# Block-causal attention with a Mish MLP: batch 0's attention from one f32 load per pair of heads, chunks of 192 tokens sharing PSUM banks, and more operations with a choice of engine

## The chip, the core and the metric

The kernel runs on one core of a Trainium2 chip. Such a core has TensorE (PE, matrix products into PSUM, with its weight loads PEld), VectorE (DVE), ScalarE (ACT), GpSimd (POOL) and SyncE (SP, which here issues every DMA). Each engine works through its own instructions in order and waits for the others at semaphores. The metric is the device time of one execution, in microseconds (us): 1071.83 for the kernel before, the median of 3 runs (1071.18 to 1075.56).

## What is computed

Eight batches of eight heads of attention over 576 tokens, with a mask of blocks of 64, and then an MLP over all 4608 tokens. Everything comes in float32, except that the two weights arrive as float64.

```python
scores = np.matmul(q, k.transpose(0, 1, 3, 2)) / np.sqrt(64)   # 8 x 8 x 576 x 576
mask = block_i >= block_j                                      # blocks of 64
scores = np.where(mask, scores, -1e9)
scores = scores - np.max(scores, axis=-1, keepdims=True)
attn = np.exp(scores)
attn = attn / (np.sum(attn, axis=-1, keepdims=True) + 1e-09)
x = np.matmul(attn, v)                # tokens x 512 after the heads are joined
h = x @ w_in                          # 512 -> 2048
g = h * np.tanh(log1p(exp(h)))        # Mish
out = g @ w_out                       # 2048 -> 512
```

## The kernel before

**Number formats.** A float32 operand is mostly split into a high and a low float16 part (`_hi`/`_lo`, `_h`/`_l`), and a product is made of three float16 ones: high by high, high by low, low by high. Some of the attention at the start is done with float32 operands on TensorE instead ("wide"). Scales that are powers of two keep the float16 parts in range: one per pair of heads for q and k (`scales`, L822), one per batch for v (`scale_x`, L686), one per group of columns for the weights (`pow2`, L448).

**Tiles.** A batch's 576 tokens are two tiles, `HALVES`, of 384 and 192 tokens. For each tile and head, `attend` (L934) does this in order:

- TensorE makes the scores with keys on the partitions, into one of two PSUM buffers `ss` (`scores(0)`, L948 to L954).
- ACT or DVE copies a first part to `mt`, and DVE takes the larger of that and the rest (`copy` L977, `larger` L989). POOL reduces over the partitions (L1021), and DVE or ACT writes the negated maximum as a row of `QB` (L1028 or L1035).
- TensorE adds a second product to the same `ss`, which subtracts the maximum (`scores(1)`), and in the float16 form also adds the low part.
- ACT takes the exponential into `pe` (L1046), POOL clears the masked corners (L1057), and for float16 ACT or DVE and then DVE split it into `p_hi` and `p_lo` (L1064, L1069, L1075).
- TensorE multiplies with v into the one PSUM bank `u` (`values` L1085; L1092 in float32, L1103 to L1105 in float16). A column of ones in v gives the row sums.
- ACT or DVE reads the sums, DVE takes the reciprocal and weighs (L1126 to L1152), and the result is split to `xt_hi` and `xt_lo` (L1163 to L1171).

When all eight heads of a tile are split, SP issues transposing DMAs (`Tile.turn`, L1206) to `x_hi` and `x_lo`. `Tile.m1` (L1217) makes the first MLP product: 16 chunks of 128 columns, 12 matmuls each, into one of three PSUM banks `acc`; ACT then writes Mish of it to `Et` (L1262), a buffer of five slots for four chunks each. `Tile.split` makes `Gt`, high and low, from a slot (L1291 to L1304). `Tile.m2` (L1316) makes the second product in four chunks of 48 matmuls, evacuates each (L1357 or L1364) and stores it (L1387).

**Loads.** `load_pair` (L733) loads q, k and v of two heads. For batch 0's first tile ("own", four pairs) they go in float32 to parts of the still unused `Et`, with k laid out twice with zeros in the other head's rows, so that each head's score product runs over all 128 rows. All other pairs, batch 0's second tile included, use two ring sets: q and k are squared and summed for the scale (ACT, L811), split (L842 to L857) and sent by 12 DMAs to the layout that the products need (L876). The first nine pairs loaded (`WIDE = 9`: four own, four for batch 0's second tile, one of batch 1) keep v and the exponentials in float32.

**Other parts at the start.** `batch` (L652) sums the squares of the batch's v for `scale_x`: four DMAs one after the other into one buffer `VL`, each followed by a square on ACT (L670, L676), then one reduction on POOL and a few DVE operations (up to L689). Every weighing waits for that. `weight` (L489) takes the float64 weights apart: DVE builds float32 from the integer words (L528, L545), ACT squares them for the scale (L556), and the high and low parts are made. For `w_in`'s first three groups (`PEW = (3, 0)`) the low part is the difference of two TensorE products with an identity (L609, L610), which `make_identity` and a negating ACT instruction (L479) prepare ahead of everything else.

**The order.** No engine order is written out by hand. Every operation is handed to a planner (`Plan.add`) with an engine, an estimated duration, its predecessors and the buffers that it takes and frees; some may go to a second engine (`other=`). `Plan.go` simulates the engines with these estimates, taking the ready operation with the earliest due time (table `DUE`), and `Plan.order` runs it backwards and forwards and keeps the best. The instructions are then emitted in the planned order, which fixes each engine's order; semaphores keep the data right. So an estimate that is too short shows as a wait in the trace, and every change of an operation can shift the order of all of them.

Of the kernel before, what the change touches and what calls it, by code (L numbers as in the profile page):

```python
# [19 lines left out]
P = 128  # L20
D = 64
EPS = 1e-9
# [7 lines left out]
    "w": ((198, 45.5, 93.5, 196.5), (118, 220.5, 212.5, 283)),  # L30
    "batch": (209, 220, 278.5, 419.5, 570, 584.5, 680, 822.5),
    "load": (
        (68, 178.5, 94, 89.5),
        (30.5, 24, 165.5, 75.5),
        (143, 130.5, 114.5, 381.5),
        (249, 231.5, 537, 626),
        (450, 465, 506, 532),
        (588, 502.5, 635.5, 628.5),
        (601, 778.5, 735, 673.5),
        (770, 742, 753.5, 656.5),  # L40
        (1259, 954, 806.5, 722.5),
    ),
    "tile": (
        (-10, 235, 68, 43, 118, 37, 41.5, 27.5,
         62.5, 140, 114, 81, 57, 122, 242.5,
         124, 242.5, 120, 204.5, 123.5, 192, 191.5),
        (183.5, 167.5, 87, 61, 129, 80.5, 91, 168.5,
         187.5, 187.5, 115, 163, 265.5, 268.5, 150,
         152, 228.5, 207, 210, 253, 206, 251),
        (103, 130, 155, 132.5, 215, 161, 223.5, 254,  # L50
         188, 203, 201, 270, 399.5, 239.5, 212,
         236, 333.5, 253, 340.5, 375.5, 275.5, 297),
        (253, 168.5, 125.5, 198.5, 289.5, 223, 331.5, 201.5,
         270.5, 394, 316, 368, 286, 369, 296.5,
         511, 308, 562.5, 417.5, 301.5, 373.5, 497.5),
        (232, 318.5, 267, 318, 322.5, 342.5, 487, 377.5,
         415.5, 371.5, 407.5, 319.5, 372.5, 377, 435,
         367.5, 415.5, 399.5, 433, 405.5, 368, 381),
        (328.5, 234, 438.5, 423, 666.5, 634.5, 798.5, 750.5,
         354, 429, 449.5, 442.5, 669.5, 602.5, 621,  # L60
         451.5, 411, 455.5, 533, 469, 648, 604.5),
        (474, 527, 530.5, 473, 536.5, 440, 425.5, 417.5,
         444, 541, 539.5, 524, 546.5, 716, 589,
         645, 449, 529.5, 520, 558, 710, 554),
        (380.5, 532.5, 342.5, 384, 451.5, 504.5, 630.5, 609,
         554, 495.5, 586.5, 512, 660.5, 538, 660.5,
         526, 612.5, 544.5, 692.5, 752.5, 760.5, 719),
        (481, 516, 610, 701.5, 676, 702, 588, 666.5,
         622, 748.5, 705, 739.5, 812.5, 655.5, 692,
         758, 790.5, 750.5, 855, 753.5, 751.5, 828.5),  # L70
        (683.5, 611.5, 574, 555.5, 764.5, 884.5, 506.5, 776,
         585, 615, 733.5, 611.5, 700.5, 680, 625,
         723, 945.5, 630.5, 737, 824, 666, 700),
        (585, 586, 612, 666.5, 620, 811.5, 578, 809,
         599.5, 541, 612.5, 626.5, 682.5, 781, 569.5,
         668.5, 655, 724.5, 657.5, 594.5, 814, 665),
        (781, 620.5, 638, 598.5, 699, 685, 692, 535,
         744.5, 796, 710, 762, 990.5, 631.5, 568,
         884, 869.5, 886, 735.5, 917, 1007, 823),
        (638.5, 1084.5, 660.5, 1071.5, 884, 798.5, 888.5, 766.5,  # L80
         586.5, 780.5, 618, 585, 843.5, 643.5, 933.5,
         766, 646.5, 875, 595, 775.5, 807, 983),
        (736.5, 605, 640.5, 609.5, 734.5, 726.5, 837, 818.5,
         882.5, 881, 857.5, 741, 963, 902, 1124.5,
         1161.5, 996, 738, 735, 794, 766, 751.5),
        (797, 835, 1111, 713.5, 806, 783.5, 943, 780.5,
         868.5, 936, 874.5, 882.5, 849.5, 863, 1069.5,
         1038, 1039, 975.5, 930, 958, 1087.5, 817.5),
        (779, 851, 790, 618.5, 759.5, 896, 933, 783,
         853, 997.5, 1080, 949, 1101, 1129, 1002.5,  # L90
         1131.5, 1065, 950, 955, 943, 989.5, 784.5),
# [4 lines left out]
class Op:  # L96


    def __init__(self, eng, us, emit, after, take, free, due, other):

        us, self.work = us if isinstance(us, tuple) else (us, 0.0)
        self.eng, self.us, self.emit = eng, us, emit
        self.ways = {eng: (us, emit)}
        if other:
# [17 lines left out]
class Plan:  # L122
# [7 lines left out]
    LAT, LATPE, OWN = 0.15, 0.2, 0.06  # L130
# [10 lines left out]

    def part(self, kind, *at):

        self.due = DUE[kind]
        for i in at:
            self.due = self.due[i]

    def add(self, eng, us, emit, after=(), take=(), free=(), other=None, table=None):
        self.ops.append(Op(eng, us, emit, after, take, free, self.due, other))
        self.ops[-1].table = table  # L150
        return self.ops[-1]

    def lat(self, a, b):
        if a.eng == "sp":
            return self.BEGIN + a.work + self.DONE
        if a.eng != b.eng or len(a.ways) > 1 or len(b.ways) > 1:
            return self.LATPE if a.eng == "pe" else self.LAT
        return 0.0 if a.eng == "pe" else self.OWN

    def go(self, due, back=False):  # L160
# [14 lines left out]
        while events:  # L175
            now = events[0][0]
            while events and events[0][0] <= now:
# [11 lines left out]
                for x in getattr(o, after):  # L189
                    j = x.i  # L190
                    lat = self.lat(x, o) if back else self.lat(o, x) * (o.eng != "sp")
# [59 lines left out]
    def order(self):  # L251
# [6 lines left out]
        _, end, _ = self.go([o.due for o in ops])  # L258
        best = None
        for _ in range(self.ROUNDS):  # L260
# [23 lines left out]
def products(ns, full=False, rows=128):  # L284

    if full:
        return sum(n / 600 + 0.07 - min(n, 320) / 9000 for n in ns), sum(n * rows / 32 for n in ns)
# [11 lines left out]
def pool(n):  # L299
    return 0.4 + n / 230  # L300
# [8 lines left out]
def attention_moe(  # L309
# [43 lines left out]
    firsts = []  # L353
    for i in range(NP):
        e = Et.rearrange("p a b c -> p (a b c)")[:, i * 1542 : (i + 1) * 1542]
        e, h = e[:, 0:Q0], e[:, Q0:]
        m = {
            "QF": e[:, 0:Q0].unsqueeze(1).to_broadcast([P, 2, Q0]),
            "KF": h[:, 0:768].rearrange("p (a s) -> p a s", a=2),
            "VF": h[:, 768 : 768 + 6 * (D + 1)].rearrange("p (c f) -> p c f", c=3),  # L360
            "Q": e[:, 0:Q0],
        }
        nc.gpsimd.memset(m["KF"][D:P, 0], 0.0)
        nc.gpsimd.memset(m["KF"][0:D, 1], 0.0)
        for j in (0, P + 1):
            nc.gpsimd.memset(m["VF"][:, :, j : j + 1], 1.0)
        firsts.append(m)
    sets = []
    for i in range(2):
        shapes = {  # L370
            "QA": [P, 2, S],
            "QB": [D + 1, 2, S],
            "KA": [P, 2, KW],
            "KB": [D + 1, 2, KW],
# [3 lines left out]
        w = 10 * (D + 1)  # L378
# [5 lines left out]
        m["VF"] = m["V"].bitcast(F32).rearrange("p (c f) -> p c f", c=5)  # L384
        nc.gpsimd.memset(m["KB"][D : D + 1], MSC)
        nc.gpsimd.memset(m["KA"][:, :, S:KW], 0.0)
        nc.gpsimd.memset(m["KB"][0:D, :, S:KW], 0.0)
        for j in (0, P + 1):
            nc.gpsimd.memset(m["VF"][:, :, j : j + 1], 1.0)
        nc.gpsimd.memset(m["VF"][64:P, 4, 1 : 1 + P], 0.0)  # L390
# [26 lines left out]
    dv, tt = room(2, "dv", [P, 6]), room(2, "tt", [P, 3, D])  # L417
    ql, kl = room(1, "ql", [P, S])[0], room(1, "kl", [P, S])[0]
# [4 lines left out]
    PW = (768, 1024)  # L423
    pe = [const.tile([P, w], F32, name=f"pe{i}") for i, w in enumerate(PW)]
    p_hi = [const.tile([P, w], F16, name=f"p_hi{i}") for i, w in enumerate(PW)]
    p_lo = [const.tile([P, w], F16, name=f"p_lo{i}") for i, w in enumerate(PW)]
# [14 lines left out]
    for t in pe[1], p_hi[1], p_lo[1]:  # L441
        nc.gpsimd.memset(t[:, 896:1024], 0.0)
# [26 lines left out]

    PEW = (3, 0)
# [5 lines left out]
    make_identity(nc, ident)  # L478
    nc.scalar.mul(minus, ident, -1.0)  # L479
# [9 lines left out]
    def weight(which, wait, room_free):  # L489
# [11 lines left out]
        last = [None] * len(raws)  # L501
        done = []
        for g in range(NG):
# [6 lines left out]
            for r in range(0, nrow, per):  # L510
# [12 lines left out]
                    [last[i]] + wait,  # L523
# [26 lines left out]
                last[i] = a  # L550
# [31 lines left out]
                other=(  # L582
# [5 lines left out]
                ),  # L588
            )
            if g < PEW[which]:  # L590
# [8 lines left out]
                    [sc] + scaled[-2],  # L599
# [52 lines left out]
    def batch(b):  # L652
# [13 lines left out]
        for i in range(4):  # L666
            d = add(
                "sp",
                dma(P * n * 4),
                lambda i=i: nc.sync.dma_start(out=flat, in_=src[:, i * n : (i + 1) * n]),  # L670
                [last.get(2)],
            )
# [3 lines left out]
                lambda i=i: nc.scalar.activation(  # L676
                    flat, flat, AF.Square, accum_out=T[:, i : i + 1]
                ),
                [d] + old,
# [11 lines left out]
        new["sx"] = add("dve", 0.6, scale_x, [red])  # L691

# [34 lines left out]


    WIDE = 9
    pair_ends = []  # L730
    last = {}

    def load_pair(b, p, q0, q1, k1, i, wait, own):  # L733
# [6 lines left out]
        nq = q1 - q0  # L740
        rows = slice(p * P, (p + 1) * P)
        nfull, rest = k1 // P, k1 % P
        nck = nfull + (rest > 0)
        wide = len(pair_ends) < WIDE
        if own:
            ts = (
                (m["Q"], qT[b, rows, q0:q1], []),
# [744 lines left out]
```

## Time and profile before

| | |
|---|---|
| time, median of 3 runs | 1071.83 us |
| the profiled execution | 1073.09 us |
| its span, first to last instruction | 1071.3 us |
| PE busy | 1009.7 us, 94% |
| DVE busy | 739.8 us, 69% |
| ACT busy | 771.2 us, 72% |
| POOL busy | 268.7 us, 25% |
| mean granted TensorE clock | 0.971 |

The profile gives each instruction's start, its duration and what ended the idle time ahead of it. On TensorE, matmuls overlap: the duration of one holds its way through the array, so a row of equal matmuls starts far more often than one lasts. The distance between starts is what a matmul costs in a dense row. The granted clock is the share of TensorE's full clock that it was given; at 0.5 a matmul takes twice as long.

### The profile page before, as it was taken

The page shows a single profiled execution, that of the slowest core. Times are in us where ns is not written, and L with a number is a line of the kernel's source. Part 1 is how long each engine was busy: PE and PEld are TensorE (multiplying, and loading weights), DVE is VectorE, ACT ScalarE, POOL GpSimd, SP SyncE. Part 2 cuts the span into 40 slices and gives each one's busy share as a digit, 9 for nine tenths or more (in the row PEclk, how much of TensorE's full clock was granted, in tenths as well). Part 3 has the DMA queues.
Part 4 walks back from the last instruction along what each step waited for, and adds up shares of the span by engine and source line. Part 5 has one row for each costly group of instructions (what it writes and reads, how often), then busy time and mean ns, then how long its engine had stood idle before and what let it go on. Part 6 is the DMA issues. An engine that isn't in the chain of part 4 may idle for free. (4 is left out here: it accounts for less than half of the span.)

```text
span 1071.3 us, 25657 instructions
## 1 busy us (share of the span) xinstructions
PE 1009.7 (94%) x9958; PEld 766.2 (72%) x9958; DVE 739.8 (69%) x1872; ACT 771.2 (72%) x1239; POOL 268.7 (25%) x410
## 2 busy tenths in 40 slices
PE   2888989989999999999999999999999998999998
PEld 1466767777776687777767687677778686767778
DVE  3888888785987578757885678746887578833500
ACT  2557887766988679867877789758887688735521
POOL 4242332241232033312431122212332133301000
PEclk7867999999999999999999999999999999999999
DMA  7767643342434433340435233441434342220100
GB/s 253 215 208 185 198 119 86 95 111 77 98 78 110 107 72 77 106 110 25 105 100 128 64 74 96 113 102 28 105 91 110 91 94 71 50 45 8 31 15 23
DMA packets 126200, 103.78 MB, mean 97 GB/s; under 512 B 51328, under 2 KB 112256, under 8 KB 126080
## 3 DMA queue, kind: packets, MB, share of 16 engines
q1 hardware_dynamic: 126080, 102.16, 36.5%
q8 instruction: 78, 1.28, 0.5%
q14 instruction: 42, 0.34, 0.1%
HBM read 56.10 MB, written 9.44 MB: 61 GB/s over the span
## 5 line engine op out<-in xcount | busy, mean ns | idle before, releaser
L1331 PE MATMUL acc<-Gt,wo_h 128*128 128x192 f16 (+1 forms) x2048 | 385.8, 287 | 1.9 <-ACT Et L1262 1.1
L1237 PE MATMUL acc<-x_lo,wi_h 128*128 128x192 f16 (+1 forms) x1024 | 295.0, 288 | 3.2 <-DMA x_lo<-xt_lo 3.2
L1237 PE MATMUL acc<-x_hi,wi_h 128*128 128x192 f16 (+1 forms) x1024 | 295.1, 288 | 2.0 <-ACT Et L1262 1.3
L1237 PE MATMUL acc<-x_hi,wi_l 128*128 128x192 f16 (+1 forms) x1024 | 295.0, 288 | 0.0
L1331 PE MATMUL acc<-Gt,wo_l 128*128 128x192 f16 (+1 forms) x1024 | 293.8, 287 | 0.0
L1021 POOL PARTITION_ALL_REDUCE mr<-mt x128 | 199.6, 1567 | 300.9 <-DVE mt L992 265.6
L1237 PEld LDWEIGHTS <-wi_h 128*128 128x128 f16 x2048 | 192.2, 98 | 77.4 <-issue 10.6
L1331 PEld LDWEIGHTS <-wo_h 128*128 128x128 f16 x2048 | 188.2, 98 | 51.2 <-issue 1.8
L1262 ACT ACTIVATE Et<-acc,bv 128x384 f32<-128x384 f32 (+1 forms) x256 | 125.5, 498 | 91.0 <-PE acc L1237 89.1
L992 DVE TENSOR_TENSOR mt<-mt,ss 128x192 f32<-128x192 f32 (+3 forms) x448 | 127.6, 297 | 13.6 <-ACT mt L979 9.2
L1304 DVE SCALAR_TENSOR_TENSOR Gt<-Et,bv,Gt 128x1536 f16<-128x1536 f32 (+1 forms) x64 | 91.5, 1431 | 54.2 <-ACT Gt L1291 54.0
L1331 PEld LDWEIGHTS <-wo_l 128*128 128x128 f16 x1024 | 100.0, 98 | 34.5 <-issue 1.3
L1237 PEld LDWEIGHTS <-wi_l 128*128 128x128 f16 x1024 | 100.4, 98 | 33.7 <-issue 1.2
L1046 ACT ACT_TABLE_LOAD x86 | 110.3, 1283 | 18.6 <-PE ss L954 8.2
L1046 ACT ACTIVATE pe<-ss,pv 128x768 f32<-128x768 f32 (+1 forms) x120 | 113.2, 956 | 7.9 <-PE ss L954 5.4
L1075 DVE TENSOR_TENSOR p_lo<-pe,p_hi 128x768 f16<-128x768 f32 (+1 forms) x108 | 113.4, 1051 | 4.5 <-ACT p_hi L1064 3.5
L1057 POOL MEMSET pe<- 64x64 f32 (+1 forms) x192 | 34.4, 210 | 318.1 <-ACT pe L1046 287.1
L1262 ACT ACT_TABLE_LOAD x87 | 111.6, 1283 | 1.5
L954 PE MATMUL ss<-QB,KB 65*128 65x192 f16 (+5 forms) x512 | 67.0, 254 | 29.9 <-POOL pv L819 13.0
L1103 PE MATMUL u<-V,p_hi 128*128 128x65 f16 x810 | 85.4, 194 | 2.1 <-DVE tt L1152 2.1
L1105 PE MATMUL u<-V,p_lo 128*128 128x65 f16 x810 | 84.7, 194 | 0.8 <-DVE p_lo L1075 0.6
L1104 PE MATMUL u<-V,p_hi 128*128 128x64 f16 x810 | 85.3, 193 | 0.0
(107 smaller groups left out, 1391.0 us busy)
## 6 DMA issues: line engine op xcount, KB each, us to landing
VL<-in_v_dram SPq DMA_DIRECT2D x32, 288.0 KB, 3.3
kl<-in_k_dram SPq DMA_DIRECT2D x32, 288.0 KB, 3.2
wo_l<-in_w_in_dram SPq DMA_DIRECT2D x8, 1024.0 KB, 5.7
Gt<-in_w_out_dram SPq DMA_DIRECT2D x16, 512.0 KB, 4.0
ql<-in_q_dram SPq DMA_DIRECT2D x28, 288.0 KB, 3.4
QA<-xh SPq DMA_DIRECT2D x112, 72.0 KB, 2.2
VL<-in_v_dram SPq DMA_DIRECT2D x27, 256.0 KB, 3.0
out_dram<-ot SPq DMA_DIRECT2D x32, 192.0 KB, 2.1
```

Of the source, the lines that this page charges most:

```text
L954: nc.tensor.matmul(ss[:, col : col + q1 - qs], lhsT=k_, rhs=q_, start=x == 0 and col % 512 == 0, stop=True, skip_group_check=True,)
L992: nc.vector.tensor_max(t, t, sv(ss_[A.slot % NSS]))
L1021: lambda: nc.gpsimd.partition_all_reduce(mr[rm][:, 0:n], mt[rm][:, 0:n], P, RED.max),
L1046: lambda: nc.scalar.activation(*spread(pe[rm], ss_[A.slot % NSS]), AF.Exp, scale=st.get("esc", D ** -0.5)),
L1075: lambda: nc.vector.tensor_sub(p_lo[rm][:, 0:W], pe[rm][:, 0:W], p_hi[rm][:, 0:W]),
L1103: nc.tensor.matmul(o, lhsT=h, rhs=vh, start=j == 0 and z == 0, stop=False)
L1104: nc.tensor.matmul(o[:, 0:D], lhsT=h, rhs=vo, start=False, stop=False)
L1105: nc.tensor.matmul(o, lhsT=l, rhs=vh, start=False, stop=end)
L1237: nc.tensor.matmul(pt[:, 0:n], lhsT=w[:, d, f * P : (f + 1) * P], rhs=x[:, d, :], start=d == 0 and z == 0, stop=d == NP - 1 and z == 2,)
L1262: nc.scalar.activation(Et[:, (self.i * NG + g) % NE, j, 0:n], acc_[c.slot % NACC][:, 0:n], AF.Mish, scale=fc[:, 0, g : g + 1])
L1304: lambda g_hi=g_hi, g_lo=g_lo, ev=ev: nc.vector.scalar_tensor_tensor(out=g_lo, in0=ev, scalar=self.s_g, in1=g_hi, op0=ALU.mult, op1=ALU.su ...
L1331: nc.tensor.matmul(pt[:, 0:n], lhsT=w[:, f, o * P : (o + 1) * P], rhs=g, start=f == 0 and z == 0, stop=f == NF - 1 and z == 2,)
```

## The change

It has these parts.

1. **Batch 0 wholly from own loads.** The own pairs now load all 576 tokens of q, k and v, and serve both tiles. The four ring loads for batch 0's second tile, with their splits and crossing DMAs, are gone, and `WIDE` with them: batch 1's first pair is float16. All of batch 0's products with own data are float32.
2. **Two heads' scores side by side.** k is laid out once, without the zeros. The two heads of a pair take one `ss` buffer each, and their products alternate, head 0 on rows 0 to 63, head 1 on rows 64 to 127.
3. **Two heads in one `u` bank.** The second head's values go beside the first's, and one set of instructions reads the sums, weighs and splits both.
4. **Chunks of 192 in pairs.** For the tiles of 192 tokens (`K = 2`) two chunks of m1 or m2 share an `acc` bank, with one Mish or one store for both.
5. **More choices of engine.** `other` is a list; casts and multiplications may go to POOL too, and for batches 0 and 1 also subtractions.
6. **The start.** The squares of batch 0's v are taken from the own loads instead of loads of their own. The identity is made inside the plan, after the reduction for `scale_x`. `PEW` is `(4, 0)`. Several clearings move from POOL to DVE.
7. **The planner.** Other estimates, a margin (`slack`, 0.7 us) between a producer and a TensorE operation from batch 1 on, another table `DUE`, and the first forward plan is also a candidate.

```diff
-            self.ways[other[0]] = other[1:]
+        for way in other:
+            self.ways[way[0]] = way[1:]
...
+            return self.BEGIN + a.work + self.DONE + b.slack
...
-    firsts = []
+    firsts, FW = [], S + KW + 5 * (P + 2)
+    Ef = Et.rearrange("p a b c -> p (a b c)")[:, 0 : NP * FW].rearrange("p (i w) -> p i w", i=NP)
...
-    PEW = (3, 0)
+    PEW = (4, 0)
...
-    make_identity(nc, ident)
-    nc.scalar.mul(minus, ident, -1.0)
...
-        for i in range(4):
-            d = add(
-                "sp",
-                dma(P * n * 4),
-                lambda i=i: nc.sync.dma_start(out=flat, in_=src[:, i * n : (i + 1) * n]),
-                [last.get(2)],
-            )
+        for i in range(NP):
+            if b:
...
+            else:
+                t_in, t_out, ds = firsts[i]["VF"][:, :, 1 : 1 + P], VL, own[i]["C"]
...
         new["sx"] = add("dve", 0.6, scale_x, [red])
+        if b == 0:
+            e = add("pool", 0.6, lambda: make_identity(nc, ident), [red])
+            last["unit"] = [
+                e,
+                add("act", act(P), lambda: nc.scalar.mul(minus, ident, -1.0), [e]),
+            ]
...
-    WIDE = 9
+    EARLY = 2
...
+            ts = ((m["QF"], qT[b, rows], []), (m["KF"][:, 0:S], kT[b, rows], []))
...
+        def scores_own():
+
+            for c, qs, col in cks:
+                for i, o in enumerate(st["rooms"]):
+                    hs = slice(i * D, (i + 1) * D)
+                    nc.tensor.matmul(
+                        ss_[o.slot % NSS][:, col : col + q1 - qs],
+                        lhsT=m["KF"][hs, c * P : (c + 1) * P],
+                        rhs=m["QF"][hs, qs:q1],
+                        start=col % 512 == 0,
+                        stop=True,
+                        skip_group_check=True,
+                    )
...
+                other=[
+                    (
+                        "pool",
+                        elem2(W),
+                        lambda: nc.gpsimd.tensor_sub(
+                            p_lo[rm][:, 0:W], pe[rm][:, 0:W], p_hi[rm][:, 0:W]
+                        ),
+                    )
+                ] if b < EARLY else [],
...
-            uv = u_[0][:, 0 : nqc * (D + 1)].rearrange("p (c f) -> p c f", f=D + 1)
+            uv = u_[0][:, 0 : nqc * 2 * E].rearrange("p (c f) -> p c f", f=2 * E)
...
-                    o = uv[:, j, :]
+                    o = uv[:, j, a * E : (a + 1) * E]
+                    begin = a == 0 and j == 0 and z == 0
...
+            self.K = Q0 // self.n
...
-            for f in range(NF):
+            K = self.K
+            for f in range(0, NF, K):
...
-            for o in range(NP):
+            for o in range(0, NP, K):
...
-    for k in range(2 * NP):
-        attend(0, k // 2, k % 2, 0, own[k // 2], k % 2)
+    for k in range(4 * NP):
+        h, p, a = k // (2 * NP), k // 2 % NP, k % 2
+        attend(0, p, a, h, own[p], a)
...
-    ring_pairs(0, Q0, (1,))
...
     for b in range(1, B):
+        plan.slack = SLACK
```

More of the change, by code (lines that the diff above doesn't have):

```diff
@@ L257, in order @@
                 o.due = min(o.due, n.due - o.us - self.lat(o, n))
-        _, end, _ = self.go([o.due for o in ops])
+        start, end, engine = self.go([o.due for o in ops])
         best = None
+        if None not in engine:
+            best = max(end), start, end, engine
         for _ in range(self.ROUNDS):
@@ L468, in pow2 @@
             )
-    PEW = (3, 0)
+    last = {}
+    PEW = (4, 0)
     scaled = [[], []]
@@ L522, in weight @@
                     ),
-                    [last[i]] + wait,
+                    [used[i]] + wait,
                 )
@@ L971, in spread @@
             )
-        A = add("pe", products(ns, own), lambda: scores(0), st["A"], take=[ss_ring])
+        if own:
+            if a == 0:
+                rooms = []
+                for _ in range(2):
+                    rooms.append(
+                        add("pe", (0.01, 0.0), lambda: None, [last.get("A")], take=[ss_ring])
+                    )
+                    last["A"] = rooms[-1]
+                st["rooms"] = rooms
+                us, work = products(ns, True)
+                st["scores"] = add(
+                    "pe", (us + 0.2, work), scores_own, st["A"] + rooms
+                )
+                last["A"] = st["scores"]
+            A, S0 = st["rooms"][a], st["scores"]
+        else:
+            A = S0 = add("pe", products(ns), lambda: scores(0), st["A"], take=[ss_ring])
+            if a:
+                C = st["u", half][0]
+                C.after.append(A)
+                A.next.append(C)
+        mx = mt[rm][:, 192 * half :]
         def copy(r, c0, c1, col):
             def op(f):
-                return lambda: f(mt[rm][r, c0:c1], ss_[A.slot % NSS][r, col + c0 : col + c1])
+                return lambda: f(mx[r, c0:c1], ss_[A.slot % NSS][r, col + c0 : col + c1])
             return add(
@@ L1107, in attend @@
         C = add(
             "pe",
-            products([D + 1] * ((1 if wide else 3) * sum(len(x) for x in blk)), wide),
+            products([E] * ((1 if own else 3) * sum(len(x) for x in blk)), own),
             values,
-            [p_in] + st["C"],
-            take=[u_ring],
-        )
-        last[p_last, rm] = [C]
-        dd, tx = dv[rm], tt[rm][:, 0:nqc, :]
-        bt = batches[b]
-        uv = u_[0][:, 0 : nqc * (D + 1)].rearrange("p (c f) -> p c f", f=D + 1)
-        before = wide and a == 0
@@ L1121, in attend @@
-        us, ux = uv[:, :, 0 if before else D], uv[:, :, before : D + before]
+            [p_in] + st["C"] + st["u", half] + [last.get("C") if own else None],
+            take=[] if a else [u_ring],
+        )
+        last[p_last, rm], last["C"] = [C], C
+        st["ends"].append(C)
+        st["u", half].append(C)
+        if a == 0:
+            return
+        wm = p % 2 if own else half
+        dd, tx = dv[wm], tt[wm][:, 0:nqc]
+        bt = batches[b]
+        uv = u_[0][:, 0 : nqc * 2 * E].rearrange("p (c f) -> p c f", f=2 * E)
@@ new lines, in m1, with prods @@
+                for k in range(K):
+                    for d in range(NP):
+                        def prods(f=f + k, k=k, d=d, parts=parts):
+                            pt = acc_[parts[0].slot % NACC][:, k * n : (k + 1) * n]
+                            for z, (w, x) in enumerate(
+                                ((wi_h, self.xh), (wi_h, self.xl), (wi_l, self.xh))
+                            ):
+                                nc.tensor.matmul(
+                                    pt,
+                                    lhsT=w[:, d, f * P : (f + 1) * P],
+                                    rhs=x[:, d, :],
+                                    start=k == 0 and d == 0 and z == 0,
+                                    stop=d == NP - 1 and z == 2,
+                                    skip_group_check=True,
+                                )
+                        begin = k == 0 and d == 0
+                        after = [chain]
+                        if begin:
+                            after = after + old[g]
+                        if f == 0 and begin:
+                            after = after + [last.get("m1")]
+                            after = after + (tiles[self.i - 2].evacs if self.i > 1 else [])
+                            after = after + self.ready
+                        if self.i < 2:
+                            after = after + w_done[0][g]
+                        chain = add(
+                            "pe", products([n] * 3), prods, after, [acc_ring] if begin else []
+                        )
+                        parts.append(chain)
```

584 lines of the change are left out of this document (286 added, 298 removed).

## The prediction

> **What bounds the kernel now.** I read the page first, then busy time by stage, then TensorE's timeline for the true pace of each product, and last the timelines of the other engines for the first 100 us.
>
> ```profile
> span 1071.3 us, 25657 instructions
> PE 1009.7 (94%) x9958; PEld 766.2 (72%) x9958; DVE 739.8 (69%) x1872; ACT 771.2 (72%) x1239; POOL 268.7 (25%) x410
> PEclk7867999999999999999999999999999999999999
> ```
>
> ```profile
> 0.00:100.00 100.00, 68.61 (x293) 47.59 (x293) 73.16 (x179) 53.42 (x106) 37.46 (x80) 0.75 0.71 217
> 100.00:200.00 100.00, 94.17 (x804) 71.81 (x805) 86.41 (x229) 82.40 (x133) 29.68 (x42) 0.94 0.46 127
> 200.00:1000.00 800.00, 778.58 (x8229) 592.53 (x8228) 568.50 (x1450) 615.85 (x968) 201.38 (x288) 1.00 0.34 85
> 1000.00:1071.30 71.30, 68.32 (x638) 54.24 (x635) 11.75 (x18) 19.51 (x35) 0.20 (x1) 1.00 0.09 25
> ```
>
> (Columns: stretch, length, then busy us and count of PE, PEld, DVE, ACT, POOL; granted clock, DMA share, GB/s.) TensorE bounds the kernel from 100 us on, and has little to do before. How little shows when busy time is replaced by pace, the distance between starts at full clock:
>
> ```profile
> 510.14 0.33 PE L1331 MATMUL acc<-Gt,wo_h 128*128 128x192 f16 x2
> ...
> 511.13 0.33 PE L1331 MATMUL acc<-Gt,wo_h 128*128 128x192 f16 x2
> ...
> 512.35 0.32 PE L1237 MATMUL acc<-x_hi,wi_h 128*128 128x384 f16 x1
> ...
> 514.30 0.33 PE L1331 MATMUL acc<-Gt,wo_h 128*128 128x192 f16 x2
> ...
> 518.24 0.19 PE L1103 MATMUL u<-V,p_hi 128*128 128x65 f16 x1
> ...
> 519.06 0.49 PE L954 MATMUL ss<-QA,KA 128*128 128x256 f16 x3
> 519.38 0.33 PE L1331 MATMUL acc<-Gt,wo_h 128*128 128x192 f16 x2
> ...
> 519.92 0.52 PE L954 MATMUL ss<-QA,KA 128*128 128x192 f16 x5
> 520.28 0.33 PE L1237 MATMUL acc<-x_hi,wi_h 128*128 128x384 f16 x1
> ```
>
> ```profile
> 40.06 1.47 PE L954 MATMUL ss<-Et 128*128 128x256 f32 x6
> 41.36 1.02 PE L609 MATMUL acc<-wo_h,p_lo 128*128 128x512 f32 x2
> ...
> 107.64 2.12 PE L1092 MATMUL u<-V,pe 128*128 128x65 f32 x18
> 109.59 0.33 PE L1237 MATMUL acc<-x_hi,wi_h 128*128 128x384 f16 x1
> ```
>
> Twelve 384-column products lie between 512.35 and 514.30, so one is paced at 0.1625 us; a 192-column one at 0.99/12 = 0.0825, an f16 value product at 0.82/27 = 0.0304. A head's f16 scores take 0.32 us (first half, 768 columns) or 0.36 (second, 832); in f32 1.30 for 768, so about 1.41 for 832. An f32 value product is two records, 1.95/9 = 0.217 us.
>
> ```profile
> L1331 PE MATMUL acc<-Gt,wo_h 128*128 128x192 f16 (+1 forms) x2048 | 385.8, 287 | 1.9 <-ACT Et L1262 1.1
> ```
>
> m1 and m2 are 3072 products of each width (this row is two thirds of m2): 499.2 + 253.4 = 752.6 us. A head of batches 1 to 7 costs 2 x 0.68 + 45 x 0.0304 = 2.73; 56 heads 152.9. Batch 0 and w_in's low parts bring the total to 967. So 104 of 1071 us are lost to idling, small gaps and the half clock. About 45 us of the work lies before 100.85, where m1 begins to run on; so **55 us are lost before that point and 49 after it**, of which the windows show 5.8 + 21.4 + 3.0 as idle.
>
> **What sets that point.**
>
> ```profile
> 7.13 5.29 PE L954 MATMUL ss<-Et 128*128 128x256 f32 x12 [7.13 <-DMA Et<-in_k_dram]
> 25.44 0.80 PE L954 MATMUL ss<-QB,KB 1*128 1x256 f16 x3 [13.03 <-POOL pv L819]
> ...
> 53.62 2.92 PE L954 MATMUL ss<-Et 128*128 128x256 f32 x6 [0.96 <-ACT pe L1046]
> ...
> 95.59 0.53 PE L1237 MATMUL acc<-x_hi,wi_h 128*128 128x384 f16 x1
> ...
> 100.85 0.53 PE L1237 MATMUL acc<-x_hi,wi_h 128*128 128x384 f16 x1
> ```
>
> ```profile
> 17.48 0.31 ACT L479 ACTIVATE p_lo<-p_lo 128x128 f16<-128x128 f32 x1 [15.46 <-POOL p_lo masks.py:199]
> ...
> 46.92 0.69 ACT L676 ACTIVATE VL<-VL 128x576 f32<-128x576 f32 x1
> ...
> 49.88 0.35 ACT L1126 ACTIVATE dv<-u,bv 128x3 f32<-128x3 f32 x1 [0.71 <-DVE bv L689]
> ```
>
> ```profile
> 17.16 0.28 POOL masks.py:199 TENSOR_SCALAR_AFFINE_SELECT p_lo<-p_lo 128x128 f32<-128x128 f32 x1 [7.19 <-issue]
> 23.46 1.44 POOL L1021 PARTITION_ALL_REDUCE mr<-mt  x1 [6.02 <-DVE mt L992]
> ...
> 63.67 4.14 POOL L1021 PARTITION_ALL_REDUCE mr<-mt  x1 [0.27 <-DVE mt L992]
> ```
>
> ```profile
> 49.69 0.15 DVE L689 TENSOR_SCALAR bv<-bv 128x1 f32<-128x1 f32 x1
> ...
> 84.82 0.35 DVE L1171 TENSOR_TENSOR xt_lo<-tt,xt_hi 128x192 f16<-128x192 f32 x1
> ```
>
> ```profile
> 42.49 0.33 SPq L670 DMA_DIRECT2D VL<-in_v_dram  x1
> ...
> 89.31 3.81 SPq L1206 DMA_TRANSPOSE x_lo<-xt_lo  x3
> ```
>
> The chain is tile 0's attention, with two delays in it that are no work. First, ACT's second instruction is the negated identity, which waits for POOL until 17.48; the copies of the first maxima queue behind it, though the scores ended at 12.42. Second, the first head's weighing (ACT L1126) waits to 49.88 for batch 0's scale (DVE L689, 49.69), since the four loads of V for the scale share one buffer and the last is issued at 42.49. Meanwhile the only `u` bank is taken, and the fifth head's scores come at 53.62. From there the last four heads need 31.55 us to 85.17, and the transposes (a w_out load and 3.81 us of issues among them) 10.4 more.
>
> **The change, part by part.**
>
> *Identity into the plan, V's sums from own tiles.* The first maxima start some 5.1 us sooner (17.6 to 12.5), and the scale needs only loads that the heads need anyway. Second scores at 25.44 - 5.1 = 20.3; three more pairs at the measured 31.55/2 = 15.8 give 67.7; transposes 10.4: m1 at 78, and the 5.3 us that lie now between its first products and its steady run make 83. I take **82**. Bounds: 72 if the pairs take 13.8 (the splitting leaves DVE), and 101 if nothing is gained. POOL's 7.19 us before the identity's select now falls behind the scale's reduction, where the max reductions of the next heads queue behind it and PE's second scores wait for those; it may be paid in full or be already covered by the loads, and the margin to 101 holds it.
>
> *Batch 0's second half in f32.* Four ring loads go, each with 12 crossing DMAs and a split; one of its DVE instructions costs 0.81 us:
>
> ```profile
> L857 DVE SCALAR_TENSOR_TENSOR xl<-kl,pv,xh 128x576 f16<-128x576 f32 x32 | 25.9, 808 | 0.1
> ```
>
> All of it lay beside the prologue, on DVE and SP, so it is priced only through the point above. In its place TensorE gets f32 scores: eight heads at 1.41 us = 11.3 if their halves of the rows run one after the other, 5.6 if side by side, against 2.9 now. No row shows two heads at once: I take 5.6, since each head has its own 64 rows and its own bank, and keep 11.3. [...]
>
> The loads that now serve both halves fill all five slots of `Et`, so m1's Mish of group g can't be written before pair g's second half has been read. At 15.8 us a pair the fourth is through at 67.7 + 63.2 = 131; from 82 to there TensorE has three groups of m1 (23.4) and the second half's 24 us of work, 47 for 49. I take **2** us of new loss, and 10 as the other end, at 17.8 us a pair.
>
> *Batch 1's first pair to f16*: 30 x 0.217 = 6.5 us become 90 x 0.0304 = 2.7. The low part of w_in's fourth group goes to TensorE, before the point, where TensorE waits anyway.
>
> So the work behind the point is 752.6 + 152.9 + batch 0's second half (5.6 + 8 x 0.36 + 72 x 0.217 = 24.1) = **930**, against 921 now.
>
> *Steady state.* The products stay as they are. Mish, evacuation, weighing and xt splits become half as many instructions in the second halves and pairs; DVE and ACT, at 71% and 77% there, get somewhat emptier, and the order leaves 0.7 us between a producer and TensorE. What that can recover is bounded by the 49 us lost, and its largest named wait is the second scores behind the written maximum:
>
> ```profile
> PE ss L954 <- ACT QB L1035: 9.3, 10, 1.6
> L1021 POOL PARTITION_ALL_REDUCE mr<-mt x128 | 199.6, 1567 | 300.9 <-DVE mt L992 265.6
> ```
>
> (The first row is for 200 us on.) I take 49 to 38: most of these 9 us and little else. Against it stands that a pair holds the one `u` bank for two heads, and that from 100 to 200 us DVE is 86% busy, so batch 1 may be late next when m1 begins sooner. Bounds 30 and 60.
>
> *Tail.* The last store carries two chunks for one, after two evacuations in place of one: a fraction of the last window's 3.0 idle us, put at nothing within a microsecond.
>
> **Sum:** 82 + 930 + 38 + 2 = 1052 us of span. The profiled execution took 1073.09 for a span of 1071.3, and the median of the runs, 1071.83, is 0.5 over that span; so **1052** stands for the median too.
>
> **Rivals.**
>
> *POOL gets in DVE's way* (1066). Casts and subtractions move to POOL, on which all 128 max reductions depend. For it: the reduction at 63.67 took 4.14 us against a mean of 1.57, beside a DVE dense with two-input instructions. Against it: POOL is 25% busy, and only early ones carry subtractions. If a quarter of a microsecond more per head reaches TensorE in 56 heads, 14 us come back. [...]
>
> *Pairs in lockstep, slower* (1083). Scores for a pair need both `ss` banks, so no third head can start until both exponentials are read. If that, and the hold on `Et`, cost what the scale's wait gives back, m1 still runs steadily only from 101; with the halves one after the other the work behind it is 936, and the losses stay at 46: 1083. It decides from a start of about 90 on. Against it: now, too, only two heads are in flight.
>
> *The heads don't run side by side* (1058): the same as the forecast with 5.7 us more.
>
> **Chances.** Forecast 0.60 (own range 1032 to 1062), side by side failing 0.10, POOL 0.15, lockstep 0.15. About 0.5% (5.4 us) can be told from no change: faster means under 1066.4. Of the POOL case half is "same"; of lockstep nearly all is slower. Faster 0.78, same 0.08, slower 0.14. Range 1026 (72 + 930 + 30, less 6 for one pair of the second half already done before m1) to 1076, most of the way to lockstep.
>
> **What would show it.** The first maxima's copy at about 12.5 us instead of 17.7; L689's counterpart before 30; m1's steady run from 75 to 90; the two heads' f32 scores starting together, 1.3 to 1.5 us a pair when warm; over 97.5% busy from 200 to 1000. The forecast is wrong if m1 starts after 90, if TensorE starves for batch 1 between 180 and 230, if Mish waits for the second half's products, or if the waits on QB grow.

## The result, and the profile after

The kernel after takes 1462.43 us, the median of 4 runs (1460.2 to 1465.7), against 1072.55 for the kernel before: a ratio of 1.363, 95% interval 1.359 to 1.367. It is 390 us slower, where 1052 was forecast, and far outside the range. No rival of the prediction comes near it.

From the page of the kernel after, the span and the busy time by engine:

```profile
span 1463.8 us, 25334 instructions
PE 1095.2 (75%) x10040; PEld 807.9 (55%) x10040; DVE 680.5 (46%) x1536; ACT 711.9 (49%) x1067; POOL 327.7 (22%) x454
PEclk6667768877788799799899989988998889989999
```

Every engine is idler than before. DVE and ACT did lose instructions, as the change meant (1872 to 1536 and 1239 to 1067), and TensorE has hardly more work, but it is busy 75% of the time instead of 94%, and its clock now sags through most of the run, to a mean granted clock of 0.857 against 0.971 before. So all engines wait, on a chain that passes through something slow. Busy time by stage of the kernel after (columns as before) shows that the loss isn't confined to the start:

```profile
0.00:100.00 100.00, 49.47 (x200) 31.80 (x200) 46.33 (x109) 33.15 (x61) 30.15 (x44) 0.66 0.55 184
...
300.00:400.00 100.00, 54.91 (x433) 38.81 (x432) 27.01 (x68) 29.71 (x45) 18.93 (x25) 0.72 0.10 28
...
1100.00:1200.00 100.00, 68.87 (x651) 50.77 (x649) 45.91 (x104) 46.41 (x76) 22.52 (x29) 0.85 0.23 63
```

The waits of TensorE and of DVE in the kernel after (engine, line, what it waited for: us in total, times, longest) lead to POOL in two steps:

```profile
PE ss L959 <- ACT QB L1078: 83.7, 12, 13.4
PE ss L959 <- DVE QB L1071: 74.5, 13, 11.5
```

```profile
DVE xl L868 <- POOL xh L860: 131.5, 21, 9.1
DVE QB L1071 <- POOL mr L1064: 130.3, 34, 13.5
```

TensorE's second scores wait for the written maximum, 158 us in all. Before, it was 16.5 us:

```profile
PE ss L954 <- ACT QB L1035: 11.5, 11, 2.2
PE ss L954 <- DVE QB L1028: 5.0, 8, 1.2
```

The maximum waits for POOL's reduction. And POOL, 22% busy, waits in turn: for other engines, as before, but for some 450 us also for none:

```profile
POOL mr L1064 <- DVE mt L1035: 217.6, 58, 16.3
...
POOL mr L1064 <- issue: 157.6, 26, 6.5
POOL xh L860 <- issue: 111.3, 15, 9.1
POOL xt_lo L1244 <- issue: 77.1, 10, 10.1
...
POOL p_lo L1124 <- issue: 35.0, 5, 7.5
```

"Issue" is time in which an engine waited for nothing that the profile shows. The prediction quoted one such row, 7.19 us ahead of the select for the identity. POOL's timeline shows what these are:

```profile
285.64 1.87 POOL L1124 TENSOR_TENSOR p_lo<-pe,p_hi 128x896 f16<-128x896 f32 x1 [7.40 <-ACT ot L1457]
293.48 0.90 POOL L1064 PARTITION_ALL_REDUCE mr<-mt  x1 [5.97 <-issue]
294.44 0.29 POOL L1100 MEMSET pe<- 64x64 f32 x2
302.26 0.66 POOL L1244 TENSOR_TENSOR xt_lo<-tt,xt_hi 128x256 f16<-128x256 f32 x1 [7.53 <-issue]
308.66 0.90 POOL L1064 PARTITION_ALL_REDUCE mr<-mt  x1 [5.75 <-issue]
```

Call it a turn when POOL goes from a reduction over partitions to a subtraction (TENSOR_TENSOR) or a multiplication (TENSOR_SCALAR), or back. On each turn to the latter it stands still for 6.7 to 10.1 us, and on each turn back for 5.7 to 6.5 (10.8 once). Going through all of POOL's timeline there are 40 turns one way and 40 back; the gaps ahead of them sum to 301 + 247 = 548 us. The row at 285.64 names another engine for its 7.40 us; that gap has the length of a turn and is counted, like 13 others put down to an engine or a DMA. Casts, clearings (MEMSET) and the identity's select leave no such gap between reductions (the 5.87 us here end a turn that began earlier):

```profile
46.64 0.44 POOL L709 PARTITION_ALL_REDUCE bv<-bv  x1 [5.87 <-issue]
46.96 0.27 POOL masks.py:197 MEMSET p_lo<- 128x128 f32 x1
47.30 0.29 POOL masks.py:199 TENSOR_SCALAR_AFFINE_SELECT p_lo<-p_lo 128x128 f32<-128x128 f32 x1
50.29 3.48 POOL L1064 PARTITION_ALL_REDUCE mr<-mt  x2 [2.69 <-DVE mt L1035]
53.64 1.02 POOL L1236 CAST xt_hi<-tt 128x384 f16<-128x384 f32 x1
54.65 0.50 POOL L826 PARTITION_ALL_REDUCE pv<-pv  x1
```

That the stop returns every time the kind changes is what these rows show. No instruction stands in the gaps; what POOL does in them, no run here shows.

### The profile page after: what moved, and what is told of

It reads as the page before. It is cut to its first block, busy times and chain, and to the rows that moved or that the text cites. A ratio compares the mean times of both kernels' runs of the same rounds, so it can differ in the third digit from the quotient of the medians.

```text
span 1463.8 us, 25334 instructions
## 1 busy us (share of the span) xinstructions
PE 1095.2 (75%) x10040; PEld 807.9 (55%) x10040; DVE 680.5 (46%) x1536; ACT 711.9 (49%) x1067; POOL 327.7 (22%) x454
## 3 DMA queue, kind: packets, MB, share of 16 engines
q8 instruction: 79, 1.29, 0.4%
## 5 line engine op out<-in xcount | busy, mean ns | idle before, releaser
L1418 PE MATMUL acc<-Gt,wo_h 128*128 128x192 f16 (+1 forms) x2048 | 415.8, 299 | 1.6 <-DVE Gt L1389 1.6
L1064 POOL PARTITION_ALL_REDUCE mr<-mt x128 | 173.0, 1364 | 400.0 <-DVE mt L1035 217.6
L959 PE MATMUL ss<-QB,KB 65*128 65x192 f16 (+7 forms) x512 | 72.6, 270 | 175.7 <-ACT QB L1078 83.7
L1342 ACT ACTIVATE Et<-acc,bv 128x384 f32<-128x384 f32 x192 | 110.2, 579 | 104.3 <-PE acc L1316 102.4
L959 PEld LDWEIGHTS <-KB 65*128 65x128 f16 (+1 forms) x512 | 44.1, 102 | 197.5 <-issue 173.2
L1146 PE MATMUL u<-V,p_hi 128*128 128x65 f16 (+1 forms) x1680 | 101.9, 200 | 40.6 <-DVE p_hi L1112 17.0
L1146 PEld LDWEIGHTS <-p_hi 128*128 128x128 f16 x1680 | 95.3, 102 | 54.0 <-DVE p_hi L1112 18.4
L1089 ACT ACTIVATE pe<-ss,pv 128x896 f32<-128x896 f32 (+1 forms) x112 | 105.8, 952 | 39.3 <-POOL p_lo L1124 19.9
L1078 ACT ACTIVATE QB<-mr 1x384 f16<-1x384 f32 (+1 forms) x75 | 33.1, 442 | 181.6 <-POOL mr L1064 181.0
L1118 DVE TENSOR_TENSOR p_lo<-pe,p_hi 128x896 f16<-128x896 f32 (+1 forms) x104 | 107.5, 1035 | 22.7 <-ACT p_hi L1107 20.8
```

Of the source, the lines that this page charges most:

```text
L959: nc.tensor.matmul(ss[:, col : col + q1 - qs], lhsT=k_[:, a, c * P : (c + 1) * P], rhs=q_[:, a, qs:q1], start=x == 0 and col % 512 == 0, s ...
L1064: lambda: nc.gpsimd.partition_all_reduce(mr[rm][:, 0:n], mx[:, 0:n], P, RED.max),
L1078: lambda: nc.scalar.mul(m["QB"][D : E, a, q0:q1], mr[rm][D : E, 0:n], -1.0 / MSC),
L1089: lambda: nc.scalar.activation(*spread(pe[rm], ss_[A.slot % NSS]), AF.Exp, scale=st.get("esc", D ** -0.5)),
L1118: lambda: nc.vector.tensor_sub(p_lo[rm][:, 0:W], pe[rm][:, 0:W], p_hi[rm][:, 0:W]),
L1146: nc.tensor.matmul(o, lhsT=l, rhs=r, start=start, stop=stop, skip_group_check=True)
```

## The experiments

Three theories stood after the traces. "Turns": the stops above are the loss. "Order": the new order, with one `u` bank for two heads and `Et` held by the loads, is the loss. "Ports", a guess that no trace shows: POOL's element work and DVE's block each other.

### No ways on POOL

Each way on POOL is deleted, casts too, and the planner orders the rest.

```diff
-                ), (
-                    "pool",
-                    elem(n),
-                    lambda j=j, n=n, src=src: nc.gpsimd.tensor_scalar_mul(
-                        xh[j][:, 0:n], src, sc[:, j : j + 1]
-                    ),
-                )],
+                )],
```

> The kernel after with no way on POOL for casts, multiplications and subtractions; the planner orders anew. Theory 'turns' (each turn of POOL between a reduction over partitions and a TENSOR_SCALAR or TENSOR_TENSOR stops it for 6 to 7.5 us; 80 turns in the kernel after): no such stop is left, time 1030 to 1075, the rest of the change as forecast. Rival 'order' (the new order, the shared u bank and Et's hold make the loss): over 1250. Rival 'ports' (POOL's element work and DVE block each other): like 'turns'.

1058.35 us; ratio to before 0.987 (0.983 to 0.990). The loss is gone, though `u`, `Et` and both `ss` banks are shared as in the kernel after. The order itself is a new one here, so this run alone doesn't rule out "order".

### Casts alone on POOL

As above, but the casts of `xt_hi` may still go to POOL.

```diff
             other=[
                 ("dve", dve(nqc * P), lambda: nc.vector.tensor_copy(out=th, in_=tx)),
                 ("pool", elem(nqc * P), lambda: nc.gpsimd.tensor_copy(out=th, in_=tx)),
             ],
...
-            other=[("pool", elem2(nqc * P), lambda: nc.gpsimd.tensor_sub(tl, tx, th))]
-            if b < EARLY
-            else [],
```

> The kernel after, where only the plain casts of xt_hi may go to POOL. 'Turns': casts followed reductions without a stop in the trace of after, so no stop, and a time within 1% of the kernel with no ways on POOL. 'Ports': some 25 us of POOL element work stay, so part of the loss does, over 1080. 'Order': over 1250.

1042.87 us; ratio 0.973 (0.970 to 0.975). This is the fastest kernel of the study together with one variant below, and 1.5% ahead of the kernel with no ways at all, a little more than the 1% expected; "ports" expected more than 1080. From its page:

```profile
span 1040.9 us, 25205 instructions
PE 1002.3 (96%) x10040; PEld 761.7 (73%) x10040; DVE 708.0 (68%) x1594; ACT 744.3 (72%) x1079; POOL 275.6 (26%) x408
```

### The same order, with DVE in POOL's place

The plan stays that of the kernel after; only what is issued for POOL's multiplications and subtractions changes.

```diff
-                        lambda: nc.gpsimd.tensor_sub(
+                        lambda: nc.vector.tensor_sub(
                             p_lo[rm][:, 0:W], pe[rm][:, 0:W], p_hi[rm][:, 0:W]
                         ),
```

> The plan and the order of the kernel after, unchanged; only the instructions planned for POOL as multiplications and subtractions are issued by DVE at the same place. 'Turns': 1050 to 1130, since some 65 us of unplanned work goes to a DVE that was 46% busy. 'Order': 1400 or more. 'Ports': like 'turns'.

1054.78 us; ratio 0.984 (0.980 to 0.988). The sharpest of these runs: the same instructions in the same planned order, and 407.7 us less than the kernel after. Over its 80 turns that is 5.1 us a turn, of the 6.9 that POOL stands still at a turn on average (548/80); the rest didn't reach the end time. It tells "turns" from "order", not yet from "ports".

### Turns forced on the kernel before

No work moved; one element is multiplied on POOL after every third reduction of maxima.

```diff
+        def reduce():
+            nc.gpsimd.partition_all_reduce(mr[rm][:, 0:n], mt[rm][:, 0:n], P, RED.max)
+            turns[0] += 1
+            if turns[0] % 3 == 0:
+                nc.gpsimd.tensor_scalar_mul(sw[1], sw[0], 2.0)
```

> The kernel before, with a one-element TENSOR_SCALAR on POOL, into a tile that nothing reads, after every third reduction of maxima: 42 of them, 84 turns, no work moved and no order changed. 'Turns': 84 stops of 6 to 7.5 us, some 570 us of POOL idle with 'issue' ahead of it, time 1300 to 1500. 'Order' and 'ports': below 1085.

1510.93 us, a little above the range expected; ratio 1.409 (1.403 to 1.415). Its POOL groups by line (busy us and mean ns, then the idle time ahead and what ended it):

```profile
L1023 POOL PARTITION_ALL_REDUCE mr<-mt x128 | 187.9, 1475 | 416.1 <-DVE mt L995 241.1 <-issue 117.0 <-DVE dv L1161 18.7
...
L822 POOL PARTITION_ALL_REDUCE pv<-pv x32 | 14.9, 466 | 140.8 <-issue 77.0 <-ACT xl L814 55.8 <-ACT Et L1272 5.8
L1026 POOL TENSOR_SCALAR sw<-sw 128x1 f32<-128x1 f32 x42 | 10.9, 260 | 303.3 <-issue 240.1 <-ACT xl L814 21.0 <-ACT Et L1272 20.9
```

42 instructions that are busy for 10.9 us in all cost 439 us, 5.2 for each of 84 turns. Instructions that are busy for 10.9 us can't block DVE for 439, so "ports" falls as the cause of the 390 us.

### Casts and few turns in the kernel before

The same place, with a cast instead; and the multiplication after every twelfth reduction only.

```diff
-                nc.gpsimd.tensor_scalar_mul(sw[1], sw[0], 2.0)
+                nc.gpsimd.tensor_copy(out=sw[1], in_=sw[0])
```

```diff
-            if turns[0] % 3 == 0:
+            if turns[0] % 12 == 0:
```

> The kernel before with a one-element cast (tensor_copy) on POOL after every third reduction of maxima, in place of the one-element multiplication that cost 439 us. [...] Rival 'any foreign instruction' (whatever stands between two reductions makes POOL start afresh): 1300 or more.

> The kernel before with the one-element multiplication after every twelfth reduction only: 10 of them, 20 turns. If each turn costs the same wherever it falls, 20 x 439/84 = 105 us, 1175 in all. Rival 'few are hidden' (other work covers a stop when the next is far away): below 1110.

The casts: 1072.63 us, ratio 0.999 (0.998 to 1.001), nothing, as "turns" has it. Its POOL groups show 42 of them with no idle time ahead:

```profile
L1026 POOL COPY sw<-sw 128x1 f32<-128x1 f32 x42 | 18.1, 431 | 0.0
```

So it is the kind of instruction, not its coming between reductions. The few turns: 1165.3 us, ratio 1.086 (1.082 to 1.090), 91.5 us for 20 turns or 4.6 each. The price is nearly proportional to the number of turns, a little lower for turns far apart.

### Two heads in turn instead of alternating

On the kernel with casts alone on POOL, with its plan:

```diff
-            for c, qs, col in cks:
-                for i, o in enumerate(st["rooms"]):
+            for i, o in enumerate(st["rooms"]):
+                for c, qs, col in cks:
```

> The kernel with casts alone on POOL, whose plan stays; the f32 scores of a pair are issued head by head instead of alternating. If alternating heads run side by side, a pair's 12 records go from 2.9 us back to about 5.3 at half clock and the 20 of the second half from 1.7 to 3.4 or less; most of it lies ahead of m1, so 1043 to 1055. If they don't overlap, no difference.

1042.14 us, ratio 0.971 (0.969 to 0.974). Neither branch of the expectation came out: there is no difference in time, and yet TensorE's timeline shows the heads overlap. First in turn, then alternating:

```profile
48.94 3.95 PE L961 MATMUL ss<-Et 64*128 64x256 f32 x12
63.77 2.72 PE L961 MATMUL ss<-Et 64*128 64x192 f32 x20
```

```profile
48.91 2.93 PE L961 MATMUL ss<-Et 64*128 64x256 f32 x12
61.72 1.79 PE L961 MATMUL ss<-Et 64*128 64x192 f32 x20
```

Such a pair takes about 1 us less when its heads alternate than in turn. The 12 records of the kernel before, with k's zeros, took 5.29 us; in turn they already take 3.95, and what makes up that part was not tried. Two of the eight pairs look different. The one at 79.22 us took 3.36, at a granted clock of 0.50, where the pair of 1.79 had 1.00. The one at 16.09 took 3.90, as in turn, though its granted clock was 0.50 like that of the pair at 48.91, and no run here tells why. The overlap saves no time here, likely because TensorE waits for written maxima among these products anyway, 22 us in all with casts alone on POOL.

### The margin, more casts, the start

All on the kernel with casts alone on POOL, each planned anew:

```diff
-    SLACK = 0.7
+    SLACK = 0.0
```

(and 0.35, and 1.0);

```diff
+                ), (
+                    "pool",
+                    elem(W),
+                    lambda: nc.gpsimd.tensor_copy(out=p_hi[rm][:, 0:W], in_=pe[rm][:, 0:W]),
                 )],
```

and, for the start,

```diff
-            if b:
+            if True:
                 d = add(
...
+    make_identity(nc, ident)
+    nc.scalar.mul(minus, ident, -1.0)
```

> The kernel with casts alone on POOL and a margin of 0 in place of 0.7 us between a producer and TensorE. If the margin is what removes TensorE's waits from 200 us on, they come back and the time is 1048 to 1056; if fewer instructions on DVE and ACT do it, 1040 to 1046.

> The kernel with casts alone on POOL and a margin of 0.35 us. If the margin itself does it, the time lies between 1043 (0.7) and 1066 (0): 1048 to 1060. If the 24 us are the scatter of one plan against another, it can fall on either side of these two.

> The kernel with casts alone on POOL and a margin of 1.0 us. If the margin itself does it, 1038 to 1046; if plans scatter, anything from 1040 to 1066.

> The kernel with casts alone on POOL, where the cast of the exponentials to p_hi may go to POOL as well. 'Turns': no stop, so POOL's work is as good as any: 1035 to 1050. 'Ports' or a POOL too busy for its reductions: above 1055.

> The kernel with casts alone on POOL, with the start as before: the identity ahead of everything, and four loads of V of their own for the scale. If the start is worth what the prediction gave it (5.1 us in the first maxima and the rest in the scale's wait), m1 starts some 15 us later and the time is 1053 to 1062. If the early heads were not held by these, 1040 to 1047.

| kernel | us | ratio to before (95%) |
|---|---|---|
| margin 0 | 1066.43 | 0.994 (0.991 to 0.996) |
| margin 0.35 | 1051.20 | 0.980 (0.977 to 0.983) |
| margin 0.7 (casts alone on POOL) | 1042.87 | 0.973 (0.970 to 0.975) |
| margin 1.0 | 1060.14 | 0.988 (0.985 to 0.991) |
| also casts to `p_hi` on POOL | 1069.77 | 0.998 (0.996 to 1.000) |
| start undone | 1066.84 | 0.994 (0.992 to 0.997) |

With the margin the time falls up to the 0.7 for which the table of due times was given and rises again behind it. At 0 it missed both branches of its expectation, slower than either; at 1.0 it fell where plans that scatter were expected. The casts to `p_hi` missed too: no turn is in that trace, and still it is 27 us slower. Since each of these runs does the same 10040 matmuls in another order, and these runs lie between 1043 and 1070, I can't tell an edit's own effect from its order's: the margin's is not shown. Whether the `p_hi` casts suffer from "ports", from a fuller POOL (340.4 us busy) or from their order stays open too.

Undoing the start costs 24 us, and there the trace shows the mechanism of a part. The identity's select comes first again, and POOL stops ahead of it and once more ahead of the first reduction, whose maxima DVE had written by 14.10:

```profile
11.76 0.28 POOL masks.py:199 TENSOR_SCALAR_AFFINE_SELECT p_lo<-p_lo 128x128 f32<-128x128 f32 x1 [9.81 <-issue]
12.10 0.52 POOL L385 MEMSET Et<- 64x512 f32 x1
20.43 2.87 POOL L1049 PARTITION_ALL_REDUCE mr<-mt  x2 [7.81 <-issue]
```

```profile
12.83 1.27 DVE L1020 TENSOR_TENSOR mt<-mt,ss 128x192 f32<-128x192 f32 x6 [4.58 <-ACT mt L1007]
```

With the start in place that reduction begins at 9.85. The scale moves as well. First DVE's write of the scale with the start undone, then with it in place:

```profile
62.12 0.15 DVE L711 TENSOR_SCALAR bv<-bv 128x1 f32<-128x1 f32 x1
```

```profile
27.91 0.15 DVE L709 TENSOR_SCALAR bv<-bv 128x1 f32<-128x1 f32 x1
```

The scale is 34 us later, the first reduction 10.6 us, and m1's first product comes at 100.82 instead of 89.97 us. These 11 us are what the trace shows of the 24; the rest may be the order's.

## Why the prediction was wrong

**The step that failed is the price of moving work to POOL.** The prediction had the row that mattered: 7.19 us of "issue" ahead of POOL's first select. It read it as a cost paid once, which "falls behind the scale's reduction". The sum has no term for POOL's casts and subtractions; they were priced only in the rival "POOL gets in DVE's way", at a quarter of a microsecond a head, 14 us in all. The bound for an operation that the trace doesn't show should have come from that row: a new kind of instruction on an engine whose last new kind stopped it for 7 us, times the number of times that the kinds alternate, up to one per reduction of maxima, of which there are 128. That end, some hundreds of us, was left out of the range. The quarter was an estimate that no run shows; in the place of its 14 us stand 80 turns at 5.1.

Before held no turn to a subtraction, as POOL did nothing there but reductions, clearings and that one select. But it likely held a second stop. Its first reduction, at 23.46, follows 6.02 us of idle time behind the select, which the view puts down to DVE; with the start undone the same place reads 7.81 us of "issue", with the maxima long written. So two kinds of instruction each had their stop in turn, and the prediction's own lines show both gaps. That the 6.02 us were a stop too is not shown for the kernel before itself.

With casts alone on POOL the select follows the scale's reduction without a stop, so the 7.19 us didn't move there. Whether a stop lies in the 7.44 us of idle time ahead of that kernel's first reduction, which end with DVE's maxima, can't be told.

**The other steps** can be judged on the three kernels without turns. With work and losses counted by the prediction's own paces:

| | forecast | no ways | casts alone | same order on DVE |
|---|---|---|---|---|
| m1's start, us | 82 | 79.2 | 90.0 | 75.7 |
| work behind it, us | 930 | 932 | 922 | 927 |
| lost behind it, us | 40 | 50 | 29 | 49 |
| span, us | 1052 | 1061.1 | 1040.9 | 1051.7 |

The measured start is m1's first product; the forecast's 82 is its steady run, with a first product at 78. That the last column comes within 1 us of the forecast is luck: it starts 6 us sooner, has 3 us less of work and loses 9 more.

- *The point at which m1 begins.* Right in size (72 to 101 given), though not along the path worked out. TensorE's timeline with casts alone on POOL:

```profile
4.55 2.93 PE L961 MATMUL ss<-Et 64*128 64x256 f32 x12 [4.55 <-DMA Et<-in_k_dram]
12.34 0.79 PE L947 MATMUL ss<-QB,KB 1*128 1x256 f16 x3 [4.86 <-ACT QB L1066]
...
89.97 0.34 PE L1292 MATMUL acc<-x_hi,wi_h 128*128 128x384 f16 x1
```

  The second scores come at 12.34, not 20.3: the first scores are also earlier and shorter, and the reduction follows at 9.85 where before it came at 23.46. In turn m1 comes late in this plan, but 922 us of work are left behind it, against 932 with no ways on POOL.
- *Batch 0's second half in f32.* The 20 records of a pair are followed 1.73 us later by the next product, 6.9 us for four pairs; 5.6 was taken, 11.3 was the other end. Right, with a term a quarter too small. The 5.6 is half of the 11.3, an estimate: measured, a pair took 1.79 us alternating and 2.72 in turn.
- *Et's hold.* 2 us were taken, 10 were the other end. TensorE waits for Mish to free an `acc` bank for 1.6 us in all with casts alone on POOL, for 6.7 with no ways and for 5.3 with the same order on DVE. Whether `Et`'s hold or Mish's place in ACT's order sets these waits wasn't tried.
- *The steady state.* A loss of 49 was to become 38, or 40 with `Et`'s 2; 29 to 50 came out. The wait on the written maximum, which was to shrink, did so in all three: from 200 us on it was 10.9 before, and 2.5, 3.2 and 3.4 here. So in two of them most of the 49 lies elsewhere. The row with casts alone on POOL, against the 9.3 that the prediction shows:

```profile
PE ss L947 <- ACT QB L1066: 3.2, 1, 3.2
```

- *Lockstep and side by side failing*, the two rivals on TensorE, did not come out: these kernels start m1 by 90 us and end ahead of 1083, and heads do overlap.

So what the change does beside POOL's turns is worth between 1.3 and 2.7%, close to the 1.8% forecast, and the turns cost 38 to 40% on top.

## What to carry to other kernels

A share of busy time says nothing on what an idle engine costs to use: before work is moved to POOL, look for rows of "issue" ahead of each new kind of instruction there, and for idle time that goes on after the inputs were written, whatever engine it is put down to. Price a turn in both directions by them, times the alternations in the planned order. A planner that knows only durations will alternate kinds whenever it helps by a few hundred nanoseconds; give it the cost of a change of kind, or offer it only kinds between which the trace shows no stop. And test a suspected cost of a kind with one-element instructions in an order that otherwise stays: 42 of them settled here what the traces only suggested.

## What the runs showed of the hardware

- Between POOL's reductions over partitions and MEMSET, CAST or COPY there was no stop, nor ahead of a select that follows reductions; in the kernel after each turn to TENSOR_SCALAR or TENSOR_TENSOR had one of 6.7 to 10.1 us (most within 7.0 to 7.7), and each turn back one of 5.7 to 6.5 (10.8 once). With one-element instructions they were 6.7 to 8.5 and 5.7 to 6.5 (9.9 once). One cast of the kernel after is an exception, at 971.35 behind a multiplication, with 5.06 us of "issue". A select that came first had 9.81 us ahead of it, and the reduction behind it 7.81.
- The stop shows no instruction and no DMA record of its own: the instruction queue q8 moved 1.29 MB with 80 turns and 1.28 MB before.
- On TensorE, f32 products on rows 0 to 63 and 64 to 127 overlap when they alternate into two banks: 1.79 us for 20 records against 2.72 in turn, both at a granted clock of 1.00. Not every pair gains: one took 3.90 us for 12 records, others 2.93.
- On TensorE, m1's 384-column products in the kernel before start 0.32 us apart between 101.17 and 102.45 us, at a granted clock of 0.50, and 0.16 apart between 105.69 and 107.47, at 1.00, where each lasts 0.33.
